# Due times for the weights that are stored ahead, and conversion buffers that are set apart one by one

## The chip, the cores and the metric

The kernel runs on one core of a Trainium2 chip. Its time is device time in microseconds (us), from one launch; three runs of the kernel before gave 951.53, 952.04 and 953.19 us, median 952.04.

## The reference, cut to what matters

Three stages in a row, in float32 (the weights are handed over as float64):

```python
# attention, batch 4, 8 heads, 576 tokens, 64 wide: q, k, v
out_d = softmax(q_d @ k_d.T / 8) @ v_d       # q_d, k_d, v_d: means over 4 neighbouring tokens
out_local = softmax(q @ k.T / 8, only |i - j| < 4) @ v
x = (repeat(out_d, 4) + out_local)           # 2304 tokens x 512
# first MLP, 512 -> 1536 -> 512
g = x @ w_gate
y = (g * sigmoid(g) * (x @ w_val)) @ w_out
# second MLP, 512 -> 2048 -> 512
h = maximum(y @ w_in, 0)
out = (h * h) @ w_out2
```

## The kernel before, in words

**Arithmetic.** Every float32 factor is split in two halves of TensorE's fast type (`fp32r`): a high half, copied by ScalarE (ACT), and a low half, the difference, formed by VectorE (DVE). A product is then three matmuls, high x high, high x low, low x high (`three`, lines 1044 to 1046). Nearly all matmuls are 128x128 by 128x256.

**Weights.** A block of weights comes as 128 x 512 float64 into a buffer `wst`, and is turned into float32 by bit operations (`bit_stages`): three passes on ACT (`sign` L366, `last_bits` L371, `scale` L375) that need a scratch buffer `bits`, then `join` on DVE (L378) into a buffer `wf`. A high half (ACT, L422 or L1346) and a low half (DVE, L425 or L1350) follow. These are called conversions here. `pair_task` converts two blocks together and combines them (DVE, L1357) into the factors of a fast 2x2 block product with seven multiplications; its results have keys `("U", q, 0..3)` or `("D", q, 0..3)`.

**Stages.** Tokens go in nine tiles of 256. Attention runs batch by batch and writes `xt` tiles (`to_x`, L724). Stage B1 takes the first six (for tiles 0 and 1 first four, later two more) of the first MLP's twelve column blocks, tile by tile: gate and value products into PSUM banks `gv`, `sg` and `hh` on DVE and ACT, then the product down into banks `y`. Stage B2 takes blocks 6 to 11 for pairs of tiles with the seven-product scheme; its unit for block j makes seven products of 6 matmuls from the factors `("U", ("f", j), ..)` (banks `gv` and `y`), forms `ss` and `h` (DVE L1736, L1789, L1792, L1799; ACT L1730, L1786, L1796), and multiplies `h` down into banks `att`, 24 matmuls. Stage C is the second MLP, in two passes over the weights `wC`.

**Weights that are stored ahead.** B1's weights stay on the core. Of the second MLP's eight blocks of weights q, those with q >= 2 are converted early (`stream`), written to DRAM (`put_task`, L444, `w_sp<-tmp`) and fetched when stage C needs them. The first four of them (`N_FIRST`, q = 4 to 7, 16 loads `wst<-wC`, L1325) go ahead of everything that stands behind them in the queue `w`: block 11 of the first MLP (also stored), then blocks 6, 7, 8, 9, 10 for B2, and the rest of the second MLP. The queue is served from its head, so blocks 6 to 10 can't begin before those sixteen loads have been issued.

**What sets the order.** The program is written out by a planner (`Order`). Each task is a list of stages with an engine, a cost, the buffers it takes and gives, and a due time. In `next` the engine whose earliest stage can start first is served, and among its stages that can start within a short look-ahead `rank` picks: those of the MLP products' chains before all others (on PE within a limit), the rest by due time. Attention tasks are due at 9 to 157.5 (batch 3's halves at 135 and 157.5), B1's own weights at 17 to 119.4. The streamed weights were due at `LATE` = 500, so every attention stage that could start went before them. Each engine, and SP's DMA queue, then executes its list in order, waiting at each instruction for its semaphores.

**The turn after attention.** The pool `att` holds attention's buffers, among them conversion buffers `bits` 1 and `tmp` 5. A planner task `late_` releases it and opens the pool `post`, which B2's weights of blocks 6 to 10 need (their first load has the condition `after([late_])`). Before, `late_` took both `bits` and all three `tmp` buffers at once, and could come when none was lent.

Of the kernel before, what the change touches and what calls it, by code (L numbers as in the profile page):

```python
# [41 lines left out]
N_FIRST, N_DIRECT, N_PUT = 4, 2, 1  # L42
# [21 lines left out]
def attn_moe_kernel(ctx: ExitStack, tc: tile.TileContext, qT, kT, vw, vin, vp, qp, kp, qs, ks, vs, maskc, masks, identc, wB, wC, out):  # L64
# [38 lines left out]
    PAD_END, PAD_WAIT, PAD_SHARE = 100.0, 0.6, 0.8  # L103
    TICK, FILL_END, BUSY = 10.24 / 3, 40.0, 3180
    W_DUE0, W_STEP, X_DUE0, X_STEP, X_STEP0 = 17.0, 2.2, 12.0, 20.0, 14.0
    CUT_T, CUT_J, W_LAG, Q_LATE, Q_LATER, MASK_PE = 2, 4, 65.0, 10.0, 6.0, 2
    V_LATE, V_LATE1, V_LATE0, V_LEAD, W_LEAD, LEAD, LATE = -15.0, -10.0, -5.0, 1000.0, 1000.0, 80.0, 500.0
    R_AT, R_STEP, LOC_LEAD, PIECE_LEAD, S_DVE, O_DVE = 3, 0.0, 60.0, 30.0, 1, 2
# [17 lines left out]
    def after(ts):  # L126

        return max([0.0] + [t.ready for t in ts]) if all(t.done for t in ts) else None
# [150 lines left out]
    order = Order()  # L279
# [69 lines left out]
    bits = [pool.tile([128, 512], I32, tag=f"bits{i}", bufs=1, name="bits") for i, pool in enumerate((com, att))]  # L349
# [105 lines left out]
    x_parts = [[] for _ in range(NT1)]  # L455
# [414 lines left out]
    att_tasks = {}  # L870
# [386 lines left out]
    for j in range(NF):  # L1257
        for i in range(3):
            due = W_DUE0 + (3 * j + i) * W_STEP + (W_LAG if j >= CUT_J else 0.0)
# [30 lines left out]
    def named(kind, n, home, i, t=0.0):  # L1290
        alias[kind, n] = home, i
        order.named[kind].append((t, n))

    def late():
        order.got["bits"].clear()
        order.got["tmp"].clear()
        order.named["tmp"] += [(0.0, 0), (0.0, 1)]
        order.named["bits"].append((0.0, 0))
        att.release()
        post = tc.alloc_tile_pool(name="post", bufs=1)  # L1300
        post_pool.append(post)
        at = after(sum(att_tasks.values(), sum(x_parts, [])))
        for kind in NAMED:
            pools[kind].append(post)
        pools["wh"][0] = post
        for n in range(2):
            named("wst", 4 + n, "bk", n)
            named("tmp", 6 + n, "bk", 2 + n)
        for kind, n in NAMED.items():
            if kind not in ("ss", "h2"):  # L1310
                order.named[kind] += [(at, i) for i in range(n[0], sum(n))]

    late_ = Task([Stage(None, 0.0, late, ("bits", "bits", "tmp", "tmp", "tmp"), cond=lambda: after(sum(att_tasks.values(), sum(x_parts, []))))])
    queues["other"].append(late_)

    stored, pairs = {}, []
# [102 lines left out]
    def keys_of(q):  # L1419
        return [(kind, q, i) for kind in "UD" for i in range(4)]  # L1420

    def stream(q):
        for kind in "UD":
            srcs = [wC[2 * q + i][:, kind == "D"] for i in range(2)]
            pair_task(kind, q, srcs, LATE, None, q >= N_DIRECT)

    def simple(fn, take, cond, queue="w"):
        queues.setdefault(queue, []).append(Task([Stage(None, 0.0, fn, take, (), cond)], LATE))
# [32 lines left out]

    simple(lend, ("wst",) * 2, lambda: after([w_tasks[j, i] for j in range(NF) for i in range(3)] + [x_tasks["B1", 3]]))
    by_need = [*range(NFP, 2 * NFP), *range(N_DIRECT, NFP), *range(N_DIRECT)]
    for q in by_need[:N_FIRST]:
        stream(q)
    ahead = [k for q in by_need[:N_FIRST] for k in keys_of(q)]

    def f_keys(j):
# [27 lines left out]
    for q in by_need[N_FIRST : 2 * NFP - N_DIRECT]:  # L1496
        stream(q)
# [9 lines left out]
    for q in by_need[2 * NFP - N_DIRECT :]:  # L1507
        stream(q)
# [926 lines left out]
```

## Time and profile before

| | |
|---|---|
| median of three runs | 952.04 us |
| the profiled execution: its time, its span | 952.56 us, 950.8 us |
| PE busy | 934.9 us, 98% of the span |
| DVE busy, ACT busy | 758.7 us (80%), 584.6 us (61%) |
| mean granted TensorE clock | 0.996 |

The span runs from the first to the last instruction; 1.76 us of the execution lie outside. PE's busy time is modelled at the ends of matmuls, so a stretch is better read by how many matmuls it holds.

### The profile page before, as it was taken

How to read it: one execution, taken by the hardware profiler on the slowest of the kernel's cores; microseconds unless marked ns; L12 is line 12 of the kernel's file. 1: busy time of each engine (PE TensorE's matmuls, PEld its weight loads, DVE VectorE, ACT ScalarE, POOL GpSimd, SP SyncE). 2: the span in 40 equal slices, each digit the busy share in tenths (PEclk: the TensorE clock that was granted, in tenths of full speed). 3: DMA queues.
4: the chain of work that ended last, by engine and by line, in shares of the span. 5: the costliest groups of instructions: out<-in, count | busy, mean ns of one | idle time of the engine just before them, and what ended most of it. 6: DMA issues, size and time to landing. Idle time of an engine off the chain costs nothing.

```text
span 950.8 us, 22582 instructions
## 1 busy us (share of the span) xinstructions
PE 934.9 (98%) x8929; PEld 909.3 (96%) x8929; DVE 758.7 (80%) x1875; ACT 584.6 (61%) x1368; POOL 23.7 (2%) x31
## 2 busy tenths in 40 slices
PE   8999999999999999899999999999999999999997
PEld 7888999999999998899999999999999999999997
DVE  7998879779877778788796989969777666776775
ACT  4878566755676787665552576757566645455453
POOL 0102102000000000000000000000000000000000
PEclk9999999999999999899999999999999999999999
DMA  9988979484777955456554547624324875426131
GB/s 295 271 281 220 246 187 254 143 267 141 238 246 259 303 175 192 147 171 214 199 169 136 175 170 279 249 104 178 112 73 171 311 225 196 158 87 244 46 133 67
DMA packets 101205, 183.82 MB, mean 193 GB/s; under 512 B 22380, under 2 KB 60012, under 8 KB 101100
## 3 DMA queue, kind: packets, MB, share of 16 engines
q1 hardware_dynamic: 97644, 174.42, 54.4%
q0 software_dynamic: 3456, 7.96, 4.7%
q8 instruction: 70, 1.15, 0.5%
q14 instruction: 35, 0.29, 0.1%
HBM read 120.75 MB, written 61.60 MB: 192 GB/s over the span
## 4 chain that ended last, share of the span: by engine, by line
PE 94%; DVE 3%; ACT 2%; DMA 0%; issue 0%; SPq 0%
PE gv L1044 11%; PE gv L1045 10%; PE gv L1046 10%; PE y L1044 8%; PE y L1045 8%; PE y L1046 8%; PE att L1974 6%; PE att L1973 6%; PE att L1972 6%; PE att L1045 3%; PE att L1046 3%; PE att L1044 3%; PE att L706 2%; PE att L648 2%; PE att L796 2%; PE y L1250 1%
## 5 line engine op out<-in xcount | busy, mean ns | idle before, releaser
L1044 PE MATMUL gv<-xs,wg 128*128 128x256 f32 x880 | 250.6, 285 | 0.6 <-DVE sg L1093 0.5
L1045 PE MATMUL gv<-xs,wg 128*128 128x256 f32 x880 | 247.0, 281 | 0.0
L1046 PE MATMUL gv<-xs,wg 128*128 128x256 f32 x880 | 246.9, 281 | 0.0
L1044 PEld LDWEIGHTS gv<-xs,wg 128*128 128x128 f32 x880 | 166.4, 189 | 3.0 <-DVE sg L1093 0.7
L1045 PEld LDWEIGHTS gv<-xs,wg 128*128 128x128 f32 x880 | 166.2, 189 | 0.0
L1046 PEld LDWEIGHTS gv<-xs,wg 128*128 128x128 f32 x880 | 166.1, 189 | 0.0
L2123 ACT ACTIVATE f<-rr 128x512 fp32r<-128x512 f32 (+2 forms) x200 | 87.8, 467 | 68.2 <-PE att L1974 32.2
L1974 PE MATMUL att<-wg,f 128*128 128x256 f32 x432 | 122.5, 284 | 0.5 <-DVE f L2126 0.4
L1972 PE MATMUL att<-wg,f 128*128 128x256 f32 x432 | 121.7, 282 | 0.3 <-ACT f L2123 0.3
L1973 PE MATMUL att<-wg,f 128*128 128x256 f32 x432 | 122.0, 282 | 0.0
L2126 DVE TENSOR_TENSOR f<-rr,f 128x512 fp32r<-128x512 f32 (+2 forms) x200 | 94.6, 490 | 29.2 <-ACT f L2123 28.2
L2047 ACT ACTIVATE rr<-rr 128x512 f32<-128x512 f32 (+1 forms) x144 | 79.8, 556 | 36.8 <-DVE rr L2050 35.1
L1045 PE MATMUL y<-xs,wg 128*128 128x256 f32 x336 | 94.7, 282 | 1.1 <-DVE xs L1562 1.1
L1044 PE MATMUL y<-xs,wg 128*128 128x256 f32 x336 | 94.6, 281 | 0.0
L1046 PE MATMUL y<-xs,wg 128*128 128x256 f32 x336 | 94.3, 281 | 0.0
L1974 PEld LDWEIGHTS att<-wg,f 128*128 128x128 f32 x432 | 81.2, 188 | 1.4 <-DVE f L2126 1.3
L1972 PEld LDWEIGHTS att<-wg,f 128*128 128x128 f32 x432 | 81.8, 189 | 0.6 <-ACT f L2123 0.6
L1973 PEld LDWEIGHTS att<-wg,f 128*128 128x128 f32 x432 | 81.5, 189 | 0.0
L2132 DVE TENSOR_TENSOR rr<-rr 128x256 f32<-128x256 f32 (+1 forms) x160 | 62.6, 393 | 9.1 <-ACT rr L2047 7.1
L1044 PE MATMUL att<-h,wg 128*128 128x256 f32 x216 | 61.9, 286 | 3.8 <-ACT h L1796 3.8
L1045 PEld LDWEIGHTS y<-xs,wg 128*128 128x128 f32 x336 | 63.5, 189 | 1.5 <-DVE xs L1562 1.5
L1044 PEld LDWEIGHTS y<-xs,wg 128*128 128x128 f32 x336 | 63.6, 189 | 0.4 <-ACT ys L1227 0.2
(149 smaller groups left out, 2326.2 us busy)
## 6 DMA issues: line engine op xcount, KB each, us to landing
wst<-wB SPq DMA_DIRECT2D x36, 512.0 KB, 4.9
w_sp<-tmp SPq DMA_DIRECT2D x36, 512.0 KB, 3.6
wg<-w_sp SPq DMA_DIRECT2D x36, 512.0 KB, 5.0
wst<-wC SPq DMA_DIRECT2D x32, 512.0 KB, 4.5
y_sp<-ys SPq DMA_DIRECT2D x29, 512.0 KB, 4.4
xf_sp<-xs SPq DMA_DIRECT2D x24, 512.0 KB, 2.7
xs<-xf_sp SPq DMA_DIRECT2D x24, 512.0 KB, 6.0
ys<-y_sp SPq DMA_DIRECT2D x20, 512.0 KB, 6.9
```

The source lines that it names most:

```text
L648: nc.tensor.matmul(u["s"][r, c * HP + hp], q[r, hp, q0 - o : q0 - o + WIN], k[r, hp, w0 - o : w0 - o + WIN], start=not mask_pe, stop=not m ...
L706: nc.tensor.matmul(ps[rr, o : o + t1 - t0], u["v"][rr, bls[c], hpp, h2, :], pt[rr, c, hpp, h2, t0 - q0 : t1 - q0], start=True, stop=True,)
L1044: nc.tensor.matmul(o, w[:, 0], x[:, 0], start=start, stop=False, skip_group_check=more)
L1045: nc.tensor.matmul(o, w[:, 0], x[:, 1], start=False, stop=False, skip_group_check=more)
L1046: nc.tensor.matmul(o, w[:, 1], x[:, 0], start=False, stop=stop, skip_group_check=more)
L1972: nc.tensor.matmul(o, h, w[:, 0], start=first and not again and c == 0, stop=False, skip_group_check=again)
L1973: nc.tensor.matmul(o, h, w[:, 1], start=False, stop=False, skip_group_check=again)
L1974: nc.tensor.matmul(o, l, w[:, 0], start=False, stop=end, skip_group_check=again)
L2047: return lambda: nc.scalar.activation(out=whole(f, c0), in_=whole(f, c0), func=func)
L2123: nc.scalar.activation(out=fac(k, 0), in_=source(), func=AF.Copy)
L2126: nc.vector.tensor_tensor(out=fac(k, 1), in0=source(), in1=fac(k, 0).bitcast(F32), op=ALU.subtract)
L2132: go = lambda: nc.vector.tensor_tensor(out=o(), in0=a(), in1=b(), op=op)
```

## The change

The streamed weights q = 4, 5, 6, 7 get due times 140, 155, 170 and 185 in place of 500. So q = 4 and 5 rank ahead of the second half of attention's last batch (157.5), and all rank by these times where nothing of the products' chains can start. The task `late_` no longer takes five buffers at once: it waits until buffer `tmp` 5 is free and drops it from the planner's list, then the same for `bits` 1, and then turns the pools, while the other `bits` and `tmp` buffers may stay lent.

```diff
+    S_DUE, S_STEP = 140.0, 15.0
...
     def late():
-        order.got["bits"].clear()
-        order.got["tmp"].clear()
-        order.named["tmp"] += [(0.0, 0), (0.0, 1)]
-        order.named["bits"].append((0.0, 0))
         att.release()
...
+    def apart(kind, n, cond=lambda: 0.0):
+        def free():
+            at = [t for t, i in order.named[kind] if i == n]
+            return max(at[0], cond()) if at and cond() is not None else None
+
+        def go():
+            order.named[kind] = [s for s in order.named[kind] if s[1] != n]
+
+        return Stage(None, 0.0, go, cond=free)
+
-    late_ = Task([Stage(None, 0.0, late, ("bits", "bits", "tmp", "tmp", "tmp"), cond=lambda: after(sum(att_tasks.values(), sum(x_parts, []))))])
+    turned_all = lambda: after(sum(att_tasks.values(), sum(x_parts, [])))
+    late_ = Task([apart("tmp", 5, turned_all), apart("bits", 1), Stage(None, 0.0, late)])
...
-    def stream(q):
+    def stream(q, due=LATE):
         for kind in "UD":
             srcs = [wC[2 * q + i][:, kind == "D"] for i in range(2)]
-            pair_task(kind, q, srcs, LATE, None, q >= N_DIRECT)
+            pair_task(kind, q, srcs, due, None, q >= N_DIRECT)
...
-    for q in by_need[:N_FIRST]:
-        stream(q)
+    for n, q in enumerate(by_need[:N_FIRST]):
+        stream(q, S_DUE + n * S_STEP)
```

The numbers of instructions on every engine stay the same. In the changed file the old lines 106 to 1294 have a number higher by one, those from 1314 on by eight. The lists are alike on every engine up to the end of attention's batch 2, and again, to the end of the program, behind the conversions for block 10 of B2's first pair of tiles. With the new due times alone, and `late_` as it was, the planner writes the same lists as with both edits; with `late_` changed alone PE's list stays as it was. What moves is shown at two places.

On SP's queue, during the window loads of attention's last batch (`vw<-vs`, 20 loads, of which the last four come further down; `wst<-wC` is a load of streamed weights, `w_sp<-tmp` a store of converted ones), there stood before:

```order
L680 DMA vw<-vs 64x4x64 x4
L444 DMA w_sp<-tmp 128x1024
L680 DMA vw<-vs 64x4x64 x4
L1325 DMA wst<-wC 128x1024
L1174 DMA y_sp<-ys 512x1x256
L680 DMA vw<-vs 64x4x64 x8
L444 DMA w_sp<-tmp 256x1x256
L1325 DMA wst<-wC 128x1024 x2
```

And on SP's queue in the changed kernel, from the same first load on:

```order
L681 DMA vw<-vs 64x4x64 x4
L1168 DMA ys<-y_sp 128x4x256
L445 DMA w_sp<-tmp 256x1x256
L1333 DMA wst<-wC 128x1024
L681 DMA vw<-vs 64x4x64 x4
L1333 DMA wst<-wC 128x1024
L1175 DMA y_sp<-ys 512x1x256
L681 DMA vw<-vs 64x4x64 x2
L445 DMA w_sp<-tmp 128x1024
L681 DMA vw<-vs 64x4x64 x2
L445 DMA w_sp<-tmp 128x1024 x2
L681 DMA vw<-vs 64x4x64 x4
```

Two loads of weights and four stores now stand ahead of the sixteenth window load, where one load and one store stood.

On ACT, at the end of the conversions for B2's blocks, before (L1730 is the first step of the unit for block 10, L1796 the high half of `h` of block 9, the rows between are block 10's conversions, of which `wh` is the last):

```order
L1730 ACTIVATE ss<-gv 128x256
L1796 ACTIVATE h_5474<-ss 128x256
L366 ACTIVATE bits<-wst 128x512
L1796 ACTIVATE h_5474<-ss 128x256
L371 ACTIVATE bits<-wst 128x512
L1346 ACTIVATE wg<-wf 128x512
L375 ACTIVATE wst<-wst 128x512
L422 ACTIVATE wg<-wf 128x512
L1346 ACTIVATE wg<-wf 128x512
L1346 ACTIVATE wh<-wf 128x256
```

And on ACT in the changed kernel (the first row is the first step of block 9, the first pair of L1804 is `h` of block 8, the second that of block 9, and the last L1738 the first step of block 10):

```order
L1738 ACTIVATE ss<-gv 128x256
L1804 ACTIVATE h_5345<-ss 128x256 x2
L1794 ACTIVATE ss<-gv 128x256
L1794 ACTIVATE ss<-ss 128x256
L1354 ACTIVATE wg<-wf 128x512
L423 ACTIVATE wg<-wf 128x512
L1354 ACTIVATE wh<-wf 128x256
L1804 ACTIVATE h_5346<-ss 128x256 x2
L1738 ACTIVATE ss<-gv 128x256
```

The last conversion for block 10, which stood behind the first step of its own unit and behind both `h` of block 9, now stands ahead of them. On PE the downward products follow this: before, those of blocks 8 and 9 stood as 24 matmuls in a row behind a single product of the next block; now they are split in twos of 12, with products of another block or pair of banks between the two.

## Rows read from the trace of the kernel before

**Rows 1.** The page, busy time of each engine.

```profile
PE 934.9 (98%) x8929; PEld 909.3 (96%) x8929; DVE 758.7 (80%) x1875; ACT 584.6 (61%) x1368; POOL 23.7 (2%) x31
```

**Rows 2.** Stretches: length, busy us (instructions) by engine, TensorE clock, DMA share, GB/s.

```profile
340.00:350.00 10.00, 10.00 (x88) 10.00 (x87) 7.28 (x18) 7.70 (x15) 0.00 (x0) 1.00 0.45 123
350.00:360.00 10.00, 8.15 (x62) 7.33 (x62) 7.67 (x17) 8.91 (x18) 0.00 (x0) 1.00 0.50 160
360.00:370.00 10.00, 10.00 (x86) 10.00 (x85) 9.14 (x23) 6.93 (x15) 0.00 (x0) 1.00 0.61 193
370.00:380.00 10.00, 8.77 (x75) 8.56 (x73) 8.31 (x21) 7.50 (x16) 0.00 (x0) 1.00 0.59 193
380.00:390.00 10.00, 8.29 (x66) 7.89 (x66) 8.46 (x20) 7.43 (x16) 0.00 (x0) 1.00 0.56 203
390.00:400.00 10.00, 8.85 (x49) 8.55 (x50) 6.61 (x15) 4.29 (x8) 0.00 (x0) 0.66 0.47 157
400.00:410.00 10.00, 10.00 (x87) 10.00 (x86) 9.08 (x23) 5.98 (x14) 0.00 (x0) 1.00 0.01 2
```

**Rows 3.** Waits of PE in the whole span: us in total, times, longest.

```profile
PE att L1044 <- ACT h L1796: 3.8, 2, 2.3
...
PE y L1045 <- DVE hh L1102: 0.8, 1, 0.8
...
PE y L1044 <- ACT ys L1227: 0.6, 1, 0.6
PE gv L1044 <- DVE sg L1093: 0.5, 1, 0.5
```

**Rows 4.** PE in order of time: start, length, line, operands, [idle before, releaser].

```profile
357.49 0.28 PE L1046 MATMUL y<-hh,wg 128*128 128x256 f32 x1
...
380.26 0.39 PE L1044 MATMUL att<-h,wg 128*128 128x256 f32 x1 [1.49 <-ACT h L1796]
...
388.44 0.28 PE L1046 MATMUL gv<-xs,wg 128*128 128x256 f32 x1
391.05 0.58 PE L1044 MATMUL att<-h,wg 128*128 128x256 f32 x1 [2.33 <-ACT h L1796]
```

**Rows 5.** ACT in order of time, first `h` of B2 and last conversion for it.

```profile
363.59 0.75 ACT L1796 ACTIVATE h<-ss 128x256 fp32r<-128x256 f32 x2
...
394.84 0.40 ACT L1346 ACTIVATE wh<-wf 128x256 fp32r<-128x256 f32 x1
```

**Rows 6.** Groups by line, 350 to 400 us: busy us, mean ns, idle before.

```profile
L366 ACT ACTIVATE bits<-wst 128x512 fp8e5<-128x512 f32 x9 | 7.0, 781 | 0.8 <-DVE wf L378 0.8
L371 ACT ACTIVATE bits<-wst 128x512 fp8e5<-128x512 uint8 x9 | 7.0, 774 | 0.0
...
L378 DVE SCALAR_TENSOR_TENSOR wf<-wst,bits 128x512 int32<-128x512 int32 x9 | 6.2, 686 | 1.1 <-ACT wst L375 1.1
L375 ACT ACTIVATE wst<-wst 128x512 f32<-128x512 f32 x9 | 6.0, 661 | 0.0
L1346 ACT ACTIVATE wg<-wf 128x512 fp32r<-128x512 f32 x9 | 5.6, 627 | 3.1 <-DVE wf L378 1.8 <-DVE wf L1357 1.3
```

**Rows 7.** Stretches of attention's last part and of B1 behind it.

```profile
170.00:270.00 100.00, 100.00 (x1185) 95.12 (x1183) 80.39 (x209) 65.53 (x164) 0.00 (x0) 1.00 0.62 200
270.00:350.00 80.00, 80.00 (x705) 79.91 (x705) 60.68 (x132) 60.08 (x120) 0.00 (x0) 1.00 0.76 256
```

**Rows 8.** SP's queue in order of time: loads of streamed weights in batch 3.

```profile
196.67 0.55 SPq L1325 DMA_DIRECT2D wst<-wC  x1
...
224.24 0.54 SPq L1325 DMA_DIRECT2D wst<-wC  x1
...
243.94 2.69 SPq L1325 DMA_DIRECT2D wst<-wC  x2
```

**Rows 9.** Waits of SP's queue, 120 to 300 us.

```profile
SPq L444 <- DVE tmp L1350: 23.6, 12, 4.3
```

**Rows 10.** DVE in order of time: attention's last write, last tile's low halves.

```profile
271.22 0.64 DVE L724 TENSOR_TENSOR xt<-att,g 128x464 f32<-128x464 f32 x1 [0.25 <-PE att L706]
...
281.92 1.29 DVE L1018 TENSOR_TENSOR xs<-xt,xs 128x512 fp32r<-128x512 f32 x2 [0.36 <-ACT xs L1014]
```

## The prediction

> **What bounds the kernel now.** I read the page first: PE is busy for 98% of the span, DVE for 80%, ACT for 61% [rows 1]. PE's idle time in the whole span is some 16 us (950.8 less 934.9); a change of order can win back that, and what a low clock costs, and little else. Next I cut the span into stretches and looked at how many matmuls each holds [rows 2]. A stretch of 10 us at full rate holds 87, that is 0.115 us for one. Those at 340 and at 400 us hold 88 and 87; the five between 350 and 400 us hold 62, 86, 75, 66 and 49. Against 87 that is 25, 1, 12, 21 and 38 too few, 97 matmuls, or 97 x 0.115 = 11.1 us. This is the largest hole in the program, and it lies at the turn from B1 to B2.
>
> What PE waits for says why. The two longest waits of that place are for `h`, 3.8 us in two waits, and three shorter ones (0.8, 0.6, 0.5 us) are for DVE and ACT work of the last B1 units [rows 3]. In order of time, the `h` waits end at 380.26 and 391.05 [rows 4]. At both the 24 matmuls of the downward product stand right behind a single product of the next block, so PE has nothing else to do while DVE and ACT make `h`. That order comes from the weights: the next block's factors were not converted when the planner had to choose. From the first `h` of B2 on ACT (363.59) to the last conversion for block 10 (394.84, with its 0.40 it ends at 395.24) [rows 5] ACT's list holds 33 conversions, 31.65 us / 33 = 0.96 us for one, while the three bit passes and the high half take 0.78, 0.77, 0.66 and 0.63 us each [rows 6]. Conversion is thus a chain that alternates with DVE and with `h`, and keeps both engines from `h` and each other.
>
> The third part is the clock. In 390 to 400 the granted clock is 0.66 of full speed, behind the two stops, and PE is idle for only 1.15 of 10 us: of the 4.4 us that are missing there (38 x 0.115) some 3.2 are matmuls at the lower of the two levels, 1.2 GHz in place of 2.4 [rows 2]. In 400 to 410 it is full again.
>
> **The change part by part.** It adds and removes no instruction, so its whole price is in the order. The lists are alike again behind block 10's conversions; whatever is won or lost has to be won by then, and the rest of the program is only shifted.
>
> The new due times. In the old lists 33 of the conversions on ACT stand behind the first `h` of B2, in the new ones 22; on DVE 34 stood behind the first sum of B2, and 25 do now. Eleven conversions on ACT by 0.96 us are 10.6 us by which block 10 is ready earlier, at about 395.2 - 10.6 = 384.6 on the old time scale. PE's first product of block 10 began six matmuls before 388.56, at about 387.9 [rows 4]; with the stops of 1.5 us at 380 and those ahead of 360 taken out it would come at about 384.5. It needs only the first of four factors, which is ready some ten conversions sooner; the last factor is needed two products (1.4 us) later. So the margin is thin for the last factor and ample for the first. For block 9, whose conversions end ahead of block 10's fourteen, it is ample. In the new list block 10's last conversion stands ahead of block 9's `h`, and the downward products are split and have other products between, so the two `h` waits should go, and with them the low clock that followed.
>
> What lies in between. The conversions that moved have to be done between 170 and 350 us. There DVE is busy for 80.4 of 100 and 60.7 of 80 us, ACT for 65.5 and 60.1 [rows 7], so 39 us of DVE and 54 of ACT are free. Nine DVE conversions by 0.69 (the join's row, the dearest kind [rows 6]) are 6.2 us, eleven on ACT by at most 0.78 are 8.6 us. They fit. There was a pause to fill, too: from 196.67 to 243.94 one streamed load only was issued (224.24) [rows 8], since batch 3's attention went first. PE shows no idle time at all in these 180 us. What added conversions cost there has bounds 0 and one short stop like those before 360 (0.5 to 0.8 us) for each of the nine, 7.2 us. I take 0.5 us, near the lower end, because DVE's share stays under 90% and PE waited for nobody at 80%. Below nothing it can't go, since there is no idle time to give back.
>
> The turn of the pools. `late_` is no instruction. It counts for nothing by itself: the new due times alone make the same lists, and with `late_` alone PE's list stays as it is. Its cost is 0, and could differ from that only through the addresses of buffers, for which no row shows a price.
>
> SP's queue. Of the moved steps the loads and stores go along: ahead of the sixteenth window load of batch 3 four stores and two weight loads stand now in place of one and one. A store waits on SP for its low half: 23.6 us in 12 waits, 4.3 at most [rows 9]. A rule of the Trainium skill speaks against the change here: "DMA: Bandwidth & Descriptors", section "Anatomy of one DMA", says that the DMA engines themselves wait on no semaphore and that the sequencer which issues a transfer holds it back; so whatever stands behind a waiting store is late. The trace agrees, as these waits stand on SP's queue. Three stores more by 4.3 us are 12.9 us at most by which the last windows could come late. Who waits for that? Attention's last write is at 271.22, the last tile's low halves end at 283.2 [rows 10]. The last tile's six units are 216 matmuls, 25 us at full rate, and end at 357.8 [rows 4], so they begin at about 332.6 or, as B2's first products stand between them, a little earlier. That leaves over 40 us. I count 0; the upper bound is the 12.9 less that store, nothing as well.
>
> The sum. The holes of 370 to 400 go: 33 + 38 matmuls, 8.2 us, and the one of 360 to 370, 0.1. Of the hole before 360 (25 matmuls, 2.9 us) I take half, 1.4 us: there the input factors of B2's first pair of tiles are formed on the same two engines, and this stays, but nine conversions fewer are left to stand between them. Less 0.5 in the attention: 8.2 + 0.1 + 1.4 - 0.5 = 9.2 us. The profiled execution took 952.56, which gives 943.4. It lies 0.5 above the median of the three runs, 952.04; against that 942.8, and I say 943.0.
>
> **The rivals.**
>
> *One stop stays.* Block 10's last factor comes a little late, a downward product waits for `h` once more, and the clock falls behind it as it did. For it: the margin of about 1.4 us. Against it: ACT and DVE have fewer other things to do, so conversions should run faster than 0.96 us. Price: one wait (2.3 us) and the low clock (3.2), 5.5 of the 9.2: 952.0 - 3.7 = 948.3.
>
> *Nothing is won, since the hole isn't made by the weights.* The seven products of the first B2 unit, its sums and `h` are one chain, and it might be this chain's start that costs. Then order alone changes nothing: 952.0. Against it: from 400 on the same units run at 87 matmuls in 10 us with DVE at 91%, once block 10 is through. For it: the wait names `h`, not a weight.
>
> *Slower: the conversions crowd attention.* The place is 200 to 270 us, where DVE had been at its fullest and where batch 3's softmax and B1's gate chain share DVE and ACT with conversions that now rank ahead of batch 3's second half. Engines run their lists in order, so a conversion that waits for ACT holds the `sg` step behind it, and PE's two `gv` banks stay taken. The price is that of the known pattern: a stop of the kind at 380 and a low clock behind it, 3.8 + 4.4 = 8.2 us an episode [rows 2]. It decides from two episodes on, which take back more than the 9.7 won: 952.0 - 9.7 + 16.4 = 958.7. For it: 80% is an average, and nine conversions come on top. Against it: PE had not a single wait here, and products' chains still rank first.
>
> *The change doesn't do what it says* is out: the lists differ as shown.
>
> **How the numbers follow.** The forecast, both `h` stops gone, gets 0.72; its own range is 941 (all 11.1 us won, none paid) to 945.5 (half of the part before 360 not won, and two short stops more). One stop left: 0.15, 948.3, between 946 and 950. Nothing won: 0.06. Slower: 0.07. Under 0.2%, 1.9 us, a measurement of this kernel can't be told from no change. So faster 0.72 + 0.15 - 0.01 = 0.86, within 0.2% 0.07, slower 0.07. For the range I leave out about 0.06 below (where later small stops go too) and 0.13 above the second case's middle: 940.5 to 948.5.
>
> **What would show it.** In the changed profile the stretches between 350 and 400 us hold 83 or more matmuls each and the clock stays at 1.00 there. PE's list of waits has no `h` wait over 1 us. Block 10's last high half on ACT (`wh`) comes near 385 us or sooner, and more streamed loads lie between 197 and 244 us. The wrong step would show as a wait of PE on `sg`, `hh` or `xs` between 170 and 350 us (crowding), a window load `vw` that PE waits for (SP's queue), or a clock under 1.00 in any stretch there. With the holes still there, the weights were not the cause.

## The result, and the profile after

The changed kernel takes 944.47 us (median of four runs, 943.21 to 945.8), the one before 952.47 in the same comparison (951.53 to 953.19): ratio 0.9917, 95% interval 0.9899 to 0.9934, about 8 us. It is faster, and inside the forecast range of 940.5 to 948.5. The profiled execution took 943.21 us with a span of 941.4, against 952.56 and 950.8: 9.4 us less, where the sum gave 9.2.

First the stretches, with columns as in [rows 2]: length, busy us and instructions of PE, its weight loads, DVE, ACT and POOL, clock, DMA share, GB/s.

```profile
350.00:360.00 10.00, 9.16 (x76) 8.77 (x75) 8.22 (x19) 9.08 (x18) 0.00 (x0) 1.00 0.52 166
360.00:370.00 10.00, 10.00 (x87) 10.00 (x86) 9.89 (x27) 8.23 (x19) 0.00 (x0) 1.00 0.92 319
370.00:380.00 10.00, 10.00 (x88) 10.00 (x87) 8.99 (x22) 7.30 (x16) 0.00 (x0) 1.00 0.52 176
380.00:390.00 10.00, 10.00 (x88) 10.00 (x87) 6.81 (x18) 3.40 (x8) 0.00 (x0) 1.00 0.32 105
390.00:400.00 10.00, 10.00 (x88) 10.00 (x87) 8.82 (x23) 5.99 (x14) 0.00 (x0) 1.00 0.01 2
```

The hole is closed from 360 us on, and the clock stays at 1.00. Of the 97 matmuls that were missing 11 still are, 87 - 76 ahead of 360 us. PE's waits, the whole list of the span (us in total, times, longest):

```profile
PE y L1251 <- ACT zeros L1245: 2.4, 1, 2.4
PE y L1046 <- DVE xs L1570: 1.1, 2, 0.6
PE y L1045 <- ACT ys L1228: 0.8, 1, 0.8
PE att L1982 <- DVE f L2134: 0.4, 1, 0.4
PE att L1980 <- ACT f L2131: 0.3, 1, 0.3
PE att L835 <- ACT pt L822: 0.2, 1, 0.2
```

Both waits for `h` are gone, and those for `hh` and `sg`; one for the copy of the last tile's result (`ys`) is left at the start of B2. On ACT, in order of time, block 10's last conversion and the first `h` behind it:

```profile
382.98 0.40 ACT L1354 ACTIVATE wh<-wf 128x256 fp32r<-128x256 f32 x1
384.05 0.76 ACT L1804 ACTIVATE h<-ss 128x256 fp32r<-128x256 f32 x2 [0.66 <-DVE ss L1800]
```

The conversion `wh` starts 11.9 us earlier than in [rows 5]. The pause of [rows 8] is filled; on SP's queue four streamed loads lie in it, where one lay:

```profile
198.46 1.18 SPq L1333 DMA_DIRECT2D wst<-wC  x2
221.80 0.33 SPq L1333 DMA_DIRECT2D wst<-wC  x1
225.25 0.54 SPq L1333 DMA_DIRECT2D wst<-wC  x1
```

And the stretches of [rows 7]: DVE and ACT have 2.6 and 3.0 us more to do in attention's last part, PE loses 0.09 us.

```profile
170.00:270.00 100.00, 99.91 (x1205) 94.92 (x1205) 83.02 (x215) 68.51 (x170) 0.00 (x0) 1.00 0.68 220
270.00:350.00 80.00, 80.00 (x682) 79.83 (x682) 63.13 (x136) 63.33 (x125) 0.00 (x0) 1.00 0.76 249
```

### The profile page after: what moved, and what is told of

Same layout as the page of the kernel before. It is cut to its first block, busy times and chain, and to the rows that moved or that the text cites. A ratio compares the mean times of both kernels' runs of the same rounds, so it can differ in the third digit from the quotient of the medians.

```text
span 941.4 us, 22569 instructions
## 1 busy us (share of the span) xinstructions
PE 931.3 (99%) x8929; PEld 906.5 (96%) x8929; DVE 758.2 (81%) x1875; ACT 583.4 (62%) x1368; POOL 23.8 (3%) x31
## 4 chain that ended last, share of the span: by engine, by line
PE 96%; DVE 2%; ACT 1%; issue 0%; DVEq 0%
PE gv L1045 11%; PE gv L1046 11%; PE gv L1047 11%; PE y L1045 8%; PE y L1046 8%; PE y L1047 8%; PE att L1982 6%; PE att L1981 6%; PE att L1980 6%; PE att L1046 3%; PE att L1047 3%; PE att L1045 3%; PE att L707 2%; PE att L649 2%; PE att L797 2%; PE y L1251 2%
## 5 line engine op out<-in xcount | busy, mean ns | idle before, releaser
L1046 PEld LDWEIGHTS y<-xs,wg 128*128 128x128 f32 x336 | 63.5, 189 | 1.5 <-DVE xs L1570 1.5
L1045 PEld LDWEIGHTS y<-xs,wg 128*128 128x128 f32 x336 | 63.6, 189 | 0.4 <-ACT ys L1228 0.2
L1047 PEld LDWEIGHTS y<-xs,wg 128*128 128x128 f32 x336 | 63.5, 189 | 0.0
```

The lines of the kernel that those rows point to most:

```text
L1045: nc.tensor.matmul(o, w[:, 0], x[:, 0], start=start, stop=False, skip_group_check=more)
L1046: nc.tensor.matmul(o, w[:, 0], x[:, 1], start=False, stop=False, skip_group_check=more)
L1047: nc.tensor.matmul(o, w[:, 1], x[:, 0], start=False, stop=stop, skip_group_check=more)
```

## The experiments

The theory is that PE's order makes the stops. Where block 9 or 10 isn't converted in time, the planner puts the downward product right behind a single product, and PE waits for the length of `h`'s chain. The rival is that the conversions themselves, as work on ACT and DVE beside `h`, make it late. A second question is what each of the two edits is worth. All runs were timed in five rounds; ratios are to the kernel before in the same rounds.

| run | median us | ratio (95% interval) |
|---|---|---|
| changed kernel again | 944.15 | 0.9902 (0.9888 to 0.9917) |
| due times alone | 949.96 | 0.9956 (0.9940 to 0.9972) |
| buffers apart alone | 952.62 | 1.0000 (0.9989 to 1.0011) |
| due times alone, fresh buffers first | 944.67 | 0.9919 (0.9906 to 0.9931) |
| changed, PE's order held | 948.75 | 0.9954 (0.9940 to 0.9969) |
| due 100 to 130, PE's order held | 947.14 | 0.9938 (0.9926 to 0.9950) |
| before, less conversion | 950.93 | 0.9978 (0.9968 to 0.9987) |
| before, stops filled | 954.86 | 1.0026 (1.0015 to 1.0037) |
| due 158 for all | 951.55 | 0.9986 (0.9974 to 0.9997) |
| due 100 to 130 | 943.65 | 0.9904 (0.9890 to 0.9919) |
| due 0 for all | 954.41 | 1.0015 (1.0006 to 1.0023) |

### The two edits apart, and the changed kernel again

The due times alone are the kernel before with the `S_DUE` lines of the change; the buffers apart alone are the changed kernel with

```diff
-        stream(q, S_DUE + n * S_STEP)
+        stream(q, LATE)
```

> Only the due times 140, 155, 170, 185; late_ takes its five buffers at once as before. The lists on all engines are the changed kernel's. If the due times alone are the cause: a ratio to before of 0.990 to 0.992, within 0.2% of the changed kernel's. If the buffers set apart have a part in it (through addresses or waits): at least 0.2% slower than the changed kernel.

> Only the conversion buffers set apart; the streamed weights due at 500 as before. PE's list is that of before, DVE's, ACT's and SP's differ a little. If the due times are the cause: ratio 0.998 to 1.002, the stretches 350 to 400 us with some 95 matmuls too few. If the turn of the pools is: 0.99 to 0.995.

> The changed kernel itself, for comparison on the same chip: ratio 0.990 to 0.993 by both theories.

The buffers apart alone change nothing, as expected; the stretches from 350 to 400 us lack 87 matmuls there (61, 86, 75, 66, 60). The due times alone bring only a third, 2.9 of 8.7 us (949.96 in place of 944.15), though the instructions stand in the same order on every engine. In their trace there is a hole that neither kernel has. Its rows in order of time (start, length, line, operands, [idle before, releaser]), first on ACT:

```profile
270.25 0.62 ACT L1347 ACTIVATE tmp<-wf 128x512 fp32r<-128x512 f32 x1
275.05 0.42 ACT L1347 ACTIVATE tmp<-wf 128x256 fp32r<-128x256 f32 x1 [4.17 <-DMA w_sp<-tmp]
```

Then on DVE:

```profile
275.50 1.03 DVE L1351 TENSOR_TENSOR tmp<-wf,tmp 128x256 fp32r<-128x256 f32 x2 [4.11 <-ACT tmp L1347]
276.44 0.41 DVE L1094 SCALAR_TENSOR_TENSOR sg<-sg,gv 128x256 f32<-128x256 f32 x1
```

On PE:

```profile
276.91 0.39 PE L1045 MATMUL gv<-xs,wg 128*128 128x256 f32 x1 [1.98 <-DVE sg L1094]
```

And the stretch, with the columns of [rows 2]:

```profile
270.00:280.00 10.00, 7.88 (x75) 7.28 (x72) 5.79 (x12) 5.83 (x13) 0.00 (x0) 1.00 0.93 325
```

Read from the end: PE waits for `sg`, which stands on DVE behind a low half, which waits for a high half on ACT, which waits 4.17 us for a store out of its own buffer. With buffer numbers and waits shown, the two programs differ just there: with the due times alone, two conversions at the turn of the pools get the buffers `tmp` 0 and 1, which hold factors still to be stored; in the changed kernel they get 6 and 7, fresh ones of the new pool, and 0 and 1 come two conversions later.

### One number in the due times alone

```diff
-        order.named["tmp"] += [(0.0, 0), (0.0, 1)]
+        order.named["tmp"] += [(0.1, 0), (0.1, 1)]
```

> The due times alone, as in the run of these alone (949.96 us), with one number changed: when late_ gives the two conversion buffers tmp 0 and 1 back to the planner's list, their free time is written as 0.1 in place of 0.0, so that the two fresh buffers of the new pool (free at 0.0) are handed out first. Lists and waits are then the changed kernel's on every engine. If the 4.2 us wait of a conversion on ACT for a store out of its buffer was what the due times alone lost: ratio to before 0.990 to 0.993, no wait of ACT for w_sp<-tmp over 1 us near 270 us. If something else of the pools (addresses) is at work: 0.994 to 0.997, as with the due times alone.

The median is 944.67 us, so with this one number the whole loss is gone, and with it the wait for the store: the loss hung on the buffers handed out at this place. The one trace of the due times alone shows 3.9 us of the 5 to 6. Ahead of the hole a matmul starts 0.7 us later than the same one in the changed kernel, behind it 3.8 us (280.78 against 277.02), and at 350 us 4.6; these last 0.8 us come from matmuls that follow each other every 118.7 ns in place of 117.3, at a granted clock of 1.00, and no view says why. That execution took 947.86 us, less than the median, at a mean clock of 0.999; five of the other six had 0.998, where the changed kernel's had 0.999 or 1.000. The old `late` gave `tmp` 0 and 1 back as free since time 0, whatever store was still under way, and the planner took them ahead of the new pool's buffers. Setting the buffers apart one by one keeps their true times, and that is what the second edit is worth: 5 to 6 us, and only with the first.

### PE's order held, conversions early

```diff
+                if name == "P6" and (key, q) in held and not all(t.at for t in held[key, q]):
+                    return None
...
+        if g == 0 and j in (8, 9):
+            held[key, ("f", j + 1)] = downs_
```

> The changed kernel, with PE's order at the two stops put back: in B2's first pair of tiles the products of blocks 9 and 10 behind the first one wait in the plan until the downward products of blocks 8 and 9 have been issued, so that these stand as 24 matmuls behind a single product again. The conversions stay early. Theory, the stops come from PE's order, which late weights force: both h waits are back with 1.5 to 2.5 us each, perhaps with the low clock; 3.5 to 7 us slower than the changed kernel, ratio to before 0.995 to 0.999. Rival, the stops come from conversions on ACT and DVE beside h: no h wait over 0.5 us, within 1 us of the changed kernel, ratio 0.991 to 0.993.

PE's waits for `h` in its trace:

```profile
PE att L1045 <- ACT h L1806: 2.8, 2, 1.5
```

And its stretches:

```profile
370.00:380.00 10.00, 8.67 (x74) 8.47 (x73) 8.99 (x23) 8.39 (x19) 0.00 (x0) 1.00 0.65 231
380.00:390.00 10.00, 9.62 (x66) 9.43 (x66) 6.08 (x16) 2.42 (x6) 0.00 (x0) 0.83 0.32 107
390.00:400.00 10.00, 8.65 (x71) 8.26 (x71) 4.55 (x13) 3.29 (x8) 0.00 (x0) 1.00 0.01 2
```

Both stops are back with 1.54 and 1.27 us, and 4.6 us of the 8.7 are lost (948.75 against 944.15), though the conversions are as early as in the changed kernel. The theory holds for both stops, but not for their whole length: the second is 1.1 us shorter than in [rows 4], the first is not. The other 4.1 us of the 8.7 don't hang on PE's order at these two places. Two parts of them can be seen: that 1.1 us, and the stretch from 350 to 360 us, which holds 75 matmuls here, 76 in the changed kernel and 62 before, 1.5 us; the rest isn't split.

### The same with the conversions out of the way

Due times 100, 110, 120, 130 and PE's order held.

> PE's order held as in the run with the stops put back, and due times 100 to 130, so that 13 conversions on ACT stand behind the first h and none of blocks 8 to 10 beside the h of blocks 8 and 9. Theory, PE's order makes the stops: both h waits are there, 1.0 to 1.5 us each, 2.5 us or more slower than with these due times and a free order (943.65). Rival, conversions beside h: no h wait over 0.5 us, within 1 us of 943.65.

PE's waits for `h`:

```profile
PE att L1045 <- ACT h L1806: 2.6, 2, 1.3
```

And the stretches behind block 10's conversions:

```profile
380.00:390.00 10.00, 8.57 (x67) 8.08 (x67) 4.52 (x13) 1.94 (x5) 0.00 (x0) 1.00 0.01 2
390.00:400.00 10.00, 9.92 (x84) 9.81 (x84) 4.61 (x13) 3.87 (x10) 0.00 (x0) 1.00 0.01 2
```

The waits end at 379.94 (1.35 us), where the last of block 10's conversions has just run, and at 389.72 (1.25 us), behind all of them: from 380 to 390 us ACT runs 5 instructions and DVE 13, and the stop is there. So about 1.3 us is the length of the chain from the last product over sum, gate and halves to `h`, less the six matmuls that cover it. By the medians 3.5 us are lost against the same due times with a free order.

### Less conversion, PE's order as before

```diff
         def sign():
             u["i"] = order.got["bits"].pop(0)
             x = upper().bitcast(F32)
+            if bare:
+                return
...
-            go = lambda: nc.vector.tensor_tensor(out=o(), in0=a(), in1=b(), op=op)
+            go = lambda: None if bare and not take else nc.vector.tensor_tensor(out=o(), in0=a(), in1=b(), op=op)
```

> The kernel before, its order kept, with less conversion for blocks 6 to 10 of the first MLP: the sign pass and the last-bits pass on ACT (30 instructions) and the three in-place combinations on DVE (15) are left out for them, so the outcome of those blocks is not the reference's. Theory, the stops come from PE's order: both h waits stay, 2.5 us or more together of the 3.8, and the time stays above 948, ratio 0.995 to 1.000. Rival, conversions beside h on ACT and DVE make the stops: the waits go, ratio 0.988 to 0.993.

PE's waits for `h`:

```profile
PE att L1048 <- ACT h L1801: 3.8, 2, 2.3
```

With 45 conversion instructions fewer the waits are 3.8 us, as before. The median fell by 2.2 us all the same (953.13 to 950.93). In the trace the `ys` wait ahead of 360 us is gone, and the low clock was shorter (0.83 from 380 to 390 us). The passes and combinations that were left out don't make the stops. But the run keeps the other conversions, and one of them stands inside the chain of the second `h`. In the kernel before, on DVE in order of time (L1792 is the last step ahead of each half of `h`, L378 the join of a conversion, L1799 a low half of `h`):

```profile
388.52 0.42 DVE L1792 SCALAR_TENSOR_TENSOR ss<-ss 128x256 f32<-128x256 f32 x1
388.86 0.42 DVE L1789 SCALAR_TENSOR_TENSOR ss<-ss 128x256 f32<-128x256 f32 x1
389.20 0.68 DVE L378 SCALAR_TENSOR_TENSOR wf<-wst,bits 128x512 int32<-128x512 int32 x1
389.80 0.41 DVE L1799 TENSOR_TENSOR h<-ss,h 128x256 fp32r<-128x256 f32 x1
390.13 0.42 DVE L1792 SCALAR_TENSOR_TENSOR ss<-ss 128x256 f32<-128x256 f32 x1
```

With less conversion the join still stands there:

```profile
390.38 0.68 DVE L382 SCALAR_TENSOR_TENSOR wf<-wst,bits 128x512 int32<-128x512 int32 x1
390.98 0.42 DVE L1804 TENSOR_TENSOR h<-ss,h 128x256 fp32r<-128x256 f32 x1
391.31 0.42 DVE L1797 SCALAR_TENSOR_TENSOR ss<-ss 128x256 f32<-128x256 f32 x1
```

With PE's order held and the conversions early, the two last steps follow each other:

```profile
390.24 0.76 DVE L1802 SCALAR_TENSOR_TENSOR ss<-ss 128x256 f32<-128x256 f32 x2
```

The join and the low half put the second step off by 0.93 us (389.20 to 390.13), and the second stop is 1.06 us longer before than with the order held. So the rival is out as the cause that there are two stops, and right for about 1 us of the second, by one conversion in DVE's list. No run moves the join alone.

### The stops filled

```diff
-                product(u[ps], factor(q, w), xh_t[key][x], start, stop, not (start or single))
+                again = {("f", 9): 2, ("f", 10): 3}.get(q, 0) if (key, name) == (("B2", 0), "P1") else 0
+                for _ in range(1 + again):
+                    product(u[ps], factor(q, w), xh_t[key][x], start, stop, not (start or single))
```

> The kernel before, with useless matmuls in its two stops: in B2's first pair of tiles the first product of block 9 is made three times over and that of block 10 four times (12 and 18 matmuls more, into the same bank, started anew each time, so with the same outcome). The conversions stay late and PE's list is otherwise that of before. If the idle time at the two stops is what lowers the clock behind them: clock 1.00 from 390 to 400 us, 2.5 to 4.5 us faster than before, ratio 0.9955 to 0.9975. If the clock falls for another reason: ratio 0.999 to 1.002.

The stretches behind the stops:

```profile
380.00:390.00 10.00, 8.81 (x73) 8.41 (x72) 7.59 (x17) 7.29 (x15) 0.00 (x0) 1.00 0.61 221
390.00:400.00 10.00, 7.18 (x54) 6.37 (x53) 7.07 (x17) 5.19 (x11) 0.00 (x0) 1.00 0.36 114
```

The time rose by 2 us, which neither expectation held. The clock stays at 1.00, as the first had it, but the stretch from 390 to 400 us holds 54 matmuls at full clock, hardly more than the 49 at the low one: PE waits there instead (`h` 2.02 us; then the factors of block 10, 0.28 and 0.22). The repeated products themselves put `h` off. They delay the first step of the next unit, which reads their bank, and on ACT this step stands ahead of the `h` that PE needs next:

```profile
392.44 0.38 ACT L1732 ACTIVATE ss<-gv 128x256 f32<-128x256 f32 x1 [2.32 <-PE gv L1046]
392.72 0.41 ACT L1798 ACTIVATE h<-ss 128x256 fp32r<-128x256 f32 x1
```

So the stops were moved more than filled, and the run doesn't price the clock. Nor does it show the stops' part in it: this trace has 1.00 in both stretches, but the mean clocks of the nine runs lie between 0.996 and 1.000, much as without the filling.

### Other due times

> The changed kernel with due time 158 for all four streamed blocks: behind all of attention, but ahead of what else is due at 500. On ACT 28 conversions stand behind the first h of B2 (33 before, 22 in the changed kernel), and only block 9's downward product stands right behind a single product. If the gain comes with every conversion done earlier: half of it, ratio 0.994 to 0.997. If it comes with the stops alone: one h wait of some 2 us is left, perhaps a low clock behind it, ratio 0.993 to 0.998, and the stretch 370 to 380 us is full.

PE's waits for `h`:

```profile
PE att L1045 <- ACT h L1804: 2.2, 1, 2.2
```

One stop is left, as expected, and the stretch from 370 to 380 us is nearly full (83 matmuls). The gain is 1.6 us by the medians (953.13 to 951.55), less than either expectation. PE waits for factors of the next block as well here (0.6 us for a high half, 0.5 in two waits for low ones), and from 380 to 400 us 38 matmuls are missing. Among the runs with a free order both stops went only where the first of these due times lay ahead of attention's last half.

> The changed kernel with due times 100, 110, 120 and 130 in place of 140 to 185, so that all four blocks rank ahead of both halves of attention's last batch. Theory, what counts is that block 10 is converted in time and not by how much: within 0.2% of the changed kernel, ratio to before 0.989 to 0.993. Rival, conversions crowd attention: stops of PE between 200 and 270 us, 2 us or more slower than the changed kernel.

It does as 140 to 185 do: 943.65 here, 944.15 and 944.47 there, the intervals overlap. No stop between 200 and 270 us. No version was found that clearly beats the changed kernel.

> The changed kernel with due time 0 for all four streamed blocks, so that their conversions rank ahead of all of attention that is left. Both theories see attention delayed here; by how much tells where crowding begins. If crowding is real: stops of PE between 200 and 235 us, 8 to 14 us together, with a low clock behind them, ratio 1.000 to 1.012. If PE's stock of B1 products covers it: ratio 0.990 to 0.995.

Crowding is real once conversions rank ahead of all attention. PE's waits from 190 to 300 us:

```profile
PE att L835 <- ACT pt L822: 2.5, 2, 1.6
PE gv L1045 <- DVE sg L1094: 1.7, 2, 1.2
```

And the stretch from 190 to 240, in which the kernel before had PE busy for 50.00 us with 681 matmuls:

```profile
190.00:240.00 50.00, 46.81 (x484) 43.24 (x484) 39.80 (x102) 35.53 (x94) 0.00 (x0) 0.97 0.84 266
```

Attention's small matmuls come late (the count falls to 484), PE runs out of products, and the time is 954.41, 10 us above the changed kernel. The two waits are 4.2 us of that, and the granted clock falls to 0.97 in the stretch; the rest isn't split. The point at which it turns lies between due times of 100 and 0.

## Why the prediction was right, and where it was not

*The hole and its size.* Right. The stretches from 360 to 400 us, 72 matmuls or 8.3 us, are full; of the part ahead of 360 us 14 of 25 matmuls came back, 1.6 us where 1.4 were put. With 9.4 us gained in the span some 0.5 were lost elsewhere, the figure that was put for the attention. One sign was set wrongly: 83 or more matmuls in each stretch can't come where the sum itself gives back half of the hole from 350 to 360 us; that stretch holds 76.

*Block 10 ready in time.* Right: 383.4 at its end, where 384.6 was worked out. Between the two rows of [rows 5] the trace has 30 conversions on ACT and not 33. That is 1.06 us for one, and 11.6 for eleven, near the 11.9 by which the last one came earlier.

*Why the stops were there.* Half right. Both reasons were given, the order that late weights force on PE and conversions that keep DVE and ACT from `h`. The runs with the order held show the first alone to make stops of 1.3 to 1.5 us, and with 45 conversions left out the waits didn't move. Conversions beside `h` show only in the second stop, 2.33 us against 1.27, and there it is one join that stands in DVE's list between the two halves of the chain.

*The clock.* The 3.2 us from 390 to 400 were counted as a loss of its own. No run takes the low clock alone away, but the runs of the kernel before that stand beside the experiments differ in it. Of these 61 the twelve with a mean clock of 0.996, that of the profiled execution, have a median of 953.17 us, and the ten with 0.999 or 1.000 one of 951.97. By these the low clock cost about 1.2 us and not 3.2, and the changed kernel is over 7 us faster than the kernel before at full clock. That is a comparison of executions and not an experiment; what PE waits for in its place at full clock isn't shown. The sum took the hole as a whole and didn't rest on this split; the price of "one stop stays" did.

*The turn of the pools.* Wrong, and it is the step that failed: "It counts for nothing by itself: the new due times alone make the same lists". The lists were the same, and the time was not. They were compared without buffer numbers and waits; with these, two conversions had other buffers, one of them under a store. The edit is worth nothing alone (1.0000) and 5 to 6 us with the new due times. The forecast survived since both edits were in the changed kernel. Had the due times come alone, 943 would have been some 7 us too low (949.96).

*SP's queue.* The answer was right: PE waits for no window load, and the last four are issued at 258.82 us, where before it was 260.17. The bound was not: from 120 to 300 us the longest wait of a store is 6.5 us, where 4.3 was taken as the most.

```profile
SPq L445 <- DVE tmp L1358: 28.7, 9, 6.5
```

*The slower rival* is a true mechanism at the wrong dose: it needs due times ahead of all attention. Its price of 8.2 us for an episode took both `h` waits (3.8 us) for one stop.

*The median* fell by 8.0 and 8.7 us in the two comparisons, the span of the profiled executions by 9.4; single runs of the kernel before lie between 951.0 and 955.8 us, so the differences are within their spread. Part of it lies at the start, which no edit touches: PE's first wait for a load (`qT`) is 0.7 us in the profiled execution before, 1.0 in the second one of the changed kernel, and not in the list of its first.

## What to carry to other kernels

A wait that names a producer can still come from the waiting engine's own list: look at what stands just ahead of the waiting instruction, and ask why the planner had nothing else to put there. Look at the producer's list too: one conversion between two steps of a chain made the second stop here 1 us longer. Compare two orders with buffer numbers and semaphores before calling them equal; a planner that gives a buffer back with a wrong free time loses what a better rank has won. Here background work could go ahead of the last part of a stage that had a stock of other work beside it, but not ahead of all that was left of it.

## What the runs showed of the hardware that was not expected

The clock behind the stops isn't the same in each execution. In profiles of three kernels that have both `h` stops it was 0.66 from 390 to 400 us in the kernel before, 0.83 from 380 to 390 with the order held, and 1.00 throughout with due times of 100 and the order held. Runs of the kernel before had a mean clock from 0.994 to 1.000 and took 955.26 and 951.04 us at these ends; the kernels without stops kept 0.999 or 1.000, and their runs lie closer together (due 100 to 130: 942.99 to 944.10; the changed kernel's first four: 943.21 to 945.80). The stops cost their own length, and in the kernel before some spread as well; the kernel with due times of 100 and the order held kept 0.999 or 1.000 in all its runs, with both stops.
